# When a kernel splits its double-precision weights: ten conversions spread over the attention, and the sign joined on another engine

## The chip, the cores and the metric

The kernel runs on one core of a Trainium2 chip. Its time is the device time of one execution in microseconds (us); lower is better. The engines are named as in the profile: PE (TensorE) multiplies matrices, with its weight loads as PEld; ACT (ScalarE) evaluates functions and copies with a scale; DVE (VectorE) and POOL (GpSimd) work element by element; SP issues DMAs. Each engine works through its own list of instructions in order and waits where an operand is not ready.

## The reference, cut to what matters

```python
def _attn_ref(q, k, v, proj):                     # 2 batches x 8 heads, 768 rows of 64
    q_bucket, k_bucket = ...                      # signs of q @ proj, k @ proj, six bits each
    mask = q_bucket[:, :, :, None] == k_bucket[:, :, None, :]
    scores = np.where(mask, scale * q @ k.T, -1e9)
    attn = softmax(scores)
    return attn @ v

def _moe_ref(x, mu_k, mu_r, w_k, w_v, w_r):       # x: 2 x 768 x 512
    xk = mu_k * x + (1.0 - mu_k) * x_prev         # x_prev: x shifted by one row
    xr = mu_r * x + (1.0 - mu_r) * x_prev
    k = np.maximum(xk @ w_k, 0.0)                 # w_k: 512 x 1024
    return sigmoid(xr @ w_r) * (k * k @ w_v)

def _moe2_ref(x, U, V, w_ch1, w_ch2):
    u = x + (x.T @ U @ V).T                       # low rank, over the rows
    return u + np.maximum(u @ w_ch1, 0.0) @ w_ch2 # w_ch1: 512 x 2048
```

The weights w_k, w_v, w_r, U, V, w_ch1 and w_ch2 come in as double precision. No engine works in it, so the kernel makes single-precision numbers of them from their two 32-bit words.

## The kernel before, in words

**Attention.** Sixteen heads of six row tiles each make 96 tiles. For a tile PE makes the scores (`scores`), DVE takes the row maximum (`row_max`), ACT the exponential (`exps`, L386, tile p), ACT or DVE the upper half of the result in 16 bits (`part1`, L393 or L391) and POOL the rest (`part2`). SP then issues a transposing DMA of both halves (`transp`, pT<-p), and PE multiplies with v (`weighted`, L416). A loop over steps n goes through a table of these operations, each with an offset, and so writes every engine's list; the first exponential comes some twelve steps in. Per head, further operations prepare q and k for the head after next: loads, transposes on PE, ACT copies (L312), DVE remainders (L317), a mask of sign bits (zt), and DMAs that put the parts together (xq, xk).

**Conversions.** A list `jobs` holds 55 blocks of weights, mostly 128 x 512. One `tick()` advances a pipeline of five stages by one block each: `conv_load` (an SP DMA of 512 KB into a buffer raw, of which there are three), `conv_scale` on ACT, `conv_bits` on DVE, `conv_sum` on POOL, and `conv_split`, which gives the upper part on ACT (L206) and the remainder on DVE (L125). A block loaded in one tick is scaled in the next and split three ticks after that. Stage `conv_scale` makes three ACT passes over the pairs of words: L168 gives a scaled copy of the high word (cx); L169 puts the low word's top three bits, as a 16-bit integer, into the low half of the low word; L170 writes the high word into the other half as a 16-bit float, scaled so far down that of it only the sign bit is left. `conv_bits` shifts cx left by three, and `conv_sum` adds the word so made.

**When the ticks run.** Ten ticks run in the attention, after the steps whose number, counted from the first step, is in `TICKS`. The others run in the layers behind it: one in each block u of 384 rows (`k_half`), of which the first layer (class Mix, once per batch) has sixteen and the second (class Channel) thirty-two per batch. In such a block PE multiplies (`k`, twelve matmuls of 384 columns), ACT and POOL square the result (L586, L587, tile sq), DVE makes its remainder (`k_low`, L592, tile hl), and PE multiplies the block before it (`v`, nine matmuls of 512 columns). The tick's first half (split and sum) stands ahead of the squares, its second half (bits, scale and load) behind them and ahead of `k_low`.

Of the kernel before, what the change touches and what calls it, by code (L numbers as in the profile page):

```python
# [11 lines left out]
F16 = mybir.dt.float16  # L12
BF16 = mybir.dt.bfloat16
AF = mybir.ActivationFunctionType
ALU = mybir.AluOpType
# [7 lines left out]
P2_DVE = ()  # L23
P1_DVE = ((0, 2), (0, 5), (1, 2), (1, 5))

TICKS = (2, 5, 7, 9, 11, 12, 13, 14, 15, 17)


DRAIN = {-4: "A", -3: "pA", -2: "A", -1: "vA", 0: "pRvR", 2: "AAvpRaR", 3: "apva", 4: "aRpa", 5: "vRa", 6: "Rvpap", 8: "Ra", 9: "va", 10: "p"}
# [39 lines left out]
]  # L69
U32 = mybir.dt.uint32  # L70
I32 = mybir.dt.int32
U16 = mybir.dt.uint16
HI_SCALE = 2.0 ** -112


# [1 line left out]
def lsh_attention_moe_kernel(  # L77
# [19 lines left out]
    nc = tc.nc  # L97
# [11 lines left out]
    scale = 1.0 / float(D) ** 0.5  # L109
# [11 lines left out]
    def f(t):  # L121
        return t.bitcast(F32)
# [26 lines left out]
    live = {}  # L149
# [13 lines left out]
    def conv_scale(j):  # L163
        d = live[j]
        r, n = d["rows"], d["n"]
        d["x"] = conv_p.tile([128, 512], F32, tag="cx", name="cx", bufs=4)[0:r, 0:n]
        half = d["raw"].bitcast(U16)
        nc.scalar.activation(d["x"], f(d["raw"])[:, :, 1], AF.Copy, scale=HI_SCALE)  # L168
        nc.scalar.activation(half[:, :, 0], d["raw"][:, :, 0], AF.Copy, scale=2.0 ** -29)  # L169
        nc.scalar.activation(half[:, :, 1].bitcast(F16), f(d["raw"])[:, :, 1], AF.Copy, scale=HI_SCALE)  # L170

    def conv_bits(j):
        x = live[j]["x"].bitcast(U32)
        nc.vector.tensor_scalar(x, x, 3, None, ALU.logical_shift_left)  # L174

    def conv_sum(j):
# [14 lines left out]
    def tick_b():  # L191
        j = tick_n[0]
        tick_n[0] += 1
        stage(j - 1, conv_bits)
        stage(j, conv_scale)
        stage(j + 1, conv_load)

    def tick():
        tick_a()
        tick_b()  # L200

    def words(w):
        return w.bitcast(U32)
# [53 lines left out]
    for s in ("q", "k"):  # L257
# [4 lines left out]
        for i, a in enumerate(sgn[s]):  # L262
# [4 lines left out]
                out=rest[r, c], in0=p_raw[r], scalar=a, in1=f(both)[r, c], op0=ALU.mult, op1=ALU.subtract  # L267
# [450 lines left out]
    for n in range(first, N + lasts + 2):  # L718
# [3 lines left out]
        for kind, off, name, *a in TABLE:  # L722
# [14 lines left out]
            else:  # L737
                j, r = divmod(n - off, 2 * NT)
                if r == 0 and 1 <= j < NH // 2:
                    fns[name](j - 1, *a)  # L740
                if n == N + END[name, a[0]]:
                    fns[name](NH // 2 - 1, *a)
        if n - first in TICKS:
            tick()
# [9 lines left out]
    low = [LowRank(0, "lr"), LowRank(1, "w_c")]  # L754
# [139 lines left out]
```

## Time and profile before

| | |
|---|---|
| median of 3 runs | 794.86 us (793.02 to 802.88) |
| the profiled execution's own time | 796.41 us |
| its span in the profile | 794.6 us |
| PE busy | 693.3 us, 87% of the span |
| ACT busy | 491.5 us, 62% |
| DVE busy | 431.8 us, 54% |
| POOL busy | 320.1 us, 40% |

The attention takes the first 310 us or so, the first layer behind it runs until 510 us, and the second until the end. An engine's share of the whole span says little here, since each stage has a limit of its own; stages are to be read one by one. All stretches are given in us from the start of the span.

### The profile page before, as it was taken

The page shows a single profiled execution, that of the slowest core. Times are in us where ns is not written, and L with a number is a line of the kernel's source. Part 1 is how long each engine was busy: PE and PEld are TensorE (multiplying, and loading weights), DVE is VectorE, ACT ScalarE, POOL GpSimd, SP SyncE. Part 2 cuts the span into 40 slices and gives each one's busy share as a digit, 9 for nine tenths or more (in the row PEclk, how much of TensorE's full clock was granted, in tenths as well). Part 3 has the DMA queues.
Part 4 walks back from the last instruction along what each step waited for, and adds up shares of the span by engine and source line. Part 5 has one row for each costly group of instructions (what it writes and reads, how often), then busy time and mean ns, then how long its engine had stood idle before and what let it go on. Part 6 is the DMA issues. An engine that isn't in the chain of part 4 may idle for free.

```text
span 794.6 us, 14578 instructions
## 1 busy us (share of the span) xinstructions
PE 693.3 (87%) x5792; PEld 604.1 (76%) x5792; DVE 431.8 (54%) x811; ACT 491.5 (62%) x685; POOL 320.1 (40%) x252
## 2 busy tenths in 40 slices
PE   4458778888788887899998899999999999999997
PEld 3347667777677776688877668788899988999996
DVE  3679868887798786555684445512433333111112
ACT  7997657766677655799947999821699521111110
POOL 1457766776777674345544544321133200000000
PEclk9559989999999999999999999999999999999999
DMA  6679999999999995033201323100234002000002
GB/s 189 176 179 219 203 187 197 204 241 196 213 201 205 199 181 81 28 116 105 65 2 53 106 85 128 54 1 26 79 112 129 27 0 80 1 1 0 1 1 79
DMA packets 180291, 86.41 MB, mean 109 GB/s; under 512 B 154432, under 2 KB 172992, under 8 KB 180224
## 3 DMA queue, kind: packets, MB, share of 16 engines
q1 hardware_dynamic: 170512, 69.36, 42.9%
q10 hardware_dynamic: 9712, 16.13, 8.5%
q8 instruction: 45, 0.74, 0.4%
q14 instruction: 22, 0.18, 0.1%
HBM read 37.10 MB, written 3.15 MB: 51 GB/s over the span
## 4 chain that ended last, share of the span: by engine, by line
PE 43%; ACT 23%; DMA 12%; DVE 10%; issue 6%; POOL 3%; ACTq 2%; SPq 0%; DVEq 0%; POOLq 0%
DMA pT<-p 9%; PE ps L603 7%; PE ps L605 7%; PE ps L604 7%; PE pt L605 6%; PE pt L603 6%; PE pt L604 6%; ACT raw L169 5%; ACT p L386 4%; ACT raw L170 3%; DVE nm L372 3%; ACT cx L168 3%; ACT w L206 2%; DVE p L391 2%; POOL p L125 2%
## 5 line engine op out<-in xcount | busy, mean ns | idle before, releaser
L125 POOL TENSOR_TENSOR p<-p,p 128x768 f16<-128x768 f32 x96 | 159.2, 1661 | 71.6 <-ACT p L393 28.6
L673 ACT ACTIVATE hl<-pt 128x384 fp32r<-128x384 f32 x64 | 31.5, 493 | 169.0 <-PE pt L605 168.9
L416 PEld LDWEIGHTS <-pT 128*128 128x128 f16 x2880 | 99.9, 99 | 37.0 <-issue 28.9
L416 PE MATMUL pt<-v,pT 128*128 128x64 bf16 (+1 forms) x2880 | 110.4, 197 | 19.2 <-DVE xn L437 14.2
L674 DVE SCALAR_TENSOR_TENSOR hl<-pt,hl 128x384 fp32r<-128x384 f32 x64 | 35.6, 557 | 160.4 <-ACT hl L673 160.4
L603 PE MATMUL ps<-w,hl 128*128 128x512 f32 x288 | 115.2, 400 | 3.9 <-ACT y L573 3.3
L125 POOL TENSOR_TENSOR cx<-cx,raw 128x512 int32<-128x512 int32 (+2 forms) x55 | 77.8, 1414 | 100.0 <-DVE cx L174 85.5
L605 PE MATMUL ps<-w,hl 128*128 128x512 f32 x288 | 114.1, 396 | 4.4 <-DVE hl L592 4.4
L386 ACT ACTIVATE p<-ps,nm 128x768 f32<-128x768 f32 x96 | 94.6, 987 | 31.0 <-DVE nm L380 14.1
L604 PE MATMUL ps<-w,hl 128*128 128x512 f32 x288 | 113.3, 393 | 0.0
L367 PE MATMUL ps<-xk,xq 76*128 76x384 f32 x192 | 76.4, 398 | 23.7 <-ACT p L386 13.3
L372 DVE TENSOR_REDUCE nm<-ps 128x1 f32<-128x768 f32 x96 | 91.5, 953 | 7.5 <-PE ps L368 6.3
L125 DVE TENSOR_TENSOR w<-cx,w 128x512 fp32r<-128x512 f32 (+2 forms) x55 | 43.5, 791 | 87.7 <-ACT w L206 87.7
L603 PE MATMUL pt<-ut,w 128*128 128x384 f32 x256 | 86.5, 338 | 0.0
L605 PE MATMUL pt<-ut,w 128*128 128x384 f32 x256 | 86.1, 336 | 0.0
L604 PE MATMUL pt<-ut,w 128*128 128x384 f32 x256 | 85.9, 336 | 0.0
L170 ACT ACTIVATE raw<-raw 128x512 f16<-128x512 f32 (+2 forms) x55 | 73.8, 1342 | 1.8
L169 ACT ACTIVATE raw<-raw 128x512 uint16<-128x512 uint32 (+2 forms) x55 | 73.3, 1333 | 0.0
L605 PEld LDWEIGHTS ps<-w,hl 128*128 128x128 f32 x288 | 54.2, 188 | 20.8 <-DVE hl L592 9.2
L393 ACT ACTIVATE p<-p 128x768 f16<-128x768 f32 x64 | 54.0, 844 | 24.7 <-DMA pT<-p 20.6
L368 PE MATMUL ps<-yk,yq 128*128 128x384 f32 x192 | 69.1, 360 | 0.0
L603 PEld LDWEIGHTS ps<-w,hl 128*128 128x128 f32 x288 | 54.2, 188 | 16.9 <-ACT y L573 4.6
(123 smaller groups left out, 1290.7 us busy)
## 6 DMA issues: line engine op xcount, KB each, us to landing
raw<-in_moe_w_ch_dram SPq DMA_DIRECT2D x32, 512.0 KB
raw<-in_moe_w_k_dram SPq DMA_DIRECT2D x8, 512.0 KB
raw<-in_moe_w_v_dram SPq DMA_DIRECT2D x8, 512.0 KB
nk<-in_k_dram ACTq DMA_DIRECT2D x16, 192.0 KB
xq<-yq ACTq DMA_DIRECT2D x16, 192.0 KB
xk<-yk ACTq DMA_DIRECT2D x16, 192.0 KB
v<-in_v_dram ACTq DMA_DIRECT2D x16, 192.0 KB
nq<-in_q_dram ACTq DMA_DIRECT2D x15, 192.0 KB
```

The source lines that it names most:

```text
L125: eng.tensor_tensor(out=out, in0=a, in1=b, op=op)
L169: nc.scalar.activation(half[:, :, 0], d["raw"][:, :, 0], AF.Copy, scale=2.0 ** -29)
L170: nc.scalar.activation(half[:, :, 1].bitcast(F16), f(d["raw"])[:, :, 1], AF.Copy, scale=HI_SCALE)
L367: nc.tensor.matmul(s_ps[:, j, 0:G], d["xq"][:, qc], d["xk"][:, c], start=True, stop=False)
L368: nc.tensor.matmul(s_ps[:, j, 0:G], d["yq"][:, qc], d["yk"][:, c], start=False, stop=True)
L372: nc.vector.tensor_reduce(out=nm[:, 0:1], in_=tl[n]["s"][:, :, 0:G], axis=AX.XY, op=ALU.max, negate=True)
L386: nc.scalar.activation(p, tl[n].pop("s")[:, :, 0:G], AF.Exp, bias=nm[:, 2:3], scale=nm[:, 1:2])
L393: nc.scalar.activation(p12[:, 0], tl[n]["p"], AF.Copy)
L416: nc.tensor.matmul(o[:, 0:d], pT[:, part, kt, :], V[a][:, kt, 0:d], start=(kt == 0 and (part, a) == (0, 1)), stop=(kt == NT - 1 and (part, ...
L603: nc.tensor.matmul(o, sh, mh, start=first, stop=False)
L604: nc.tensor.matmul(o, sh, ml, start=False, stop=False)
L605: nc.tensor.matmul(o, sl, mh, start=False, stop=last)
```

## The change

Two things change. First, the ten ticks of the attention run after steps 2, 5, 8, 22, 32, and so on to 82, so three of them run in the first steps and seven are ten steps apart. Second, `conv_scale` loses its third pass. Its second pass now writes the low word's top three bits as a 32-bit integer over the low word, and a new DVE instruction at the head of `conv_bits` masks the sign out of the high word and ORs it into the low word.

```diff
-TICKS = (2, 5, 7, 9, 11, 12, 13, 14, 15, 17)
+TICKS = (2, 5, 8, 22, 32, 42, 52, 62, 72, 82)
...
-U16 = mybir.dt.uint16
...
-        half = d["raw"].bitcast(U16)
+        low = d["raw"][:, :, 0]
         nc.scalar.activation(d["x"], f(d["raw"])[:, :, 1], AF.Copy, scale=HI_SCALE)
-        nc.scalar.activation(half[:, :, 0], d["raw"][:, :, 0], AF.Copy, scale=2.0 ** -29)
-        nc.scalar.activation(half[:, :, 1].bitcast(F16), f(d["raw"])[:, :, 1], AF.Copy, scale=HI_SCALE)
+        nc.scalar.activation(low, low, AF.Copy, scale=2.0 ** -29)
...
     def conv_bits(j):
-        x = live[j]["x"].bitcast(U32)
+        x, raw = words(live[j]["x"]), live[j]["raw"]
+        nc.vector.scalar_tensor_tensor(
+            out=raw[:, :, 0], in0=raw[:, :, 1], scalar=0x80000000, in1=raw[:, :, 0],
+            op0=ALU.bitwise_and, op1=ALU.bitwise_or,
+        )
         nc.vector.tensor_scalar(x, x, 3, None, ALU.logical_shift_left)
```

The lines of the changed kernel are numbered anew: the passes are L167 and L168, the new DVE instruction is L172 and the shift L176. Lines further on are two higher than before, those of the helper L125 one lower.

On ACT, up to the second exponential (L386), these rows stand before; the conversions are L168 to L170, and L206 is the split.

```order
L325 DMA xk<-yk 64x768
L206 ACTIVATE w<-cx 128x512
L168 ACTIVATE cx<-raw 128x512
L169 ACTIVATE raw<-raw 128x512
L170 ACTIVATE raw<-raw 128x512
L386 ACTIVATE p<-ps,nm 128x768
L237 DMA v_0_126<-in_v_dram 128x384
L393 ACTIVATE p_286<-p 128x768
L312 ACTIVATE yk<-pt 64x3x128 x2
L206 ACTIVATE w<-cx 128x512
L168 ACTIVATE cx<-raw 128x512
L169 ACTIVATE raw<-raw 128x512
```

At the same place on ACT there stands now:

```order
L327 DMA xk<-yk 64x768
L388 ACTIVATE p<-ps,nm 128x768
L239 DMA v_0_126<-in_v_dram 128x384
L395 ACTIVATE p_263<-p 128x768
L314 ACTIVATE yk<-pt 64x3x128 x2
L239 DMA nk<-in_k_dram 128x384
L388 ACTIVATE p<-ps,nm 128x768
L395 ACTIVATE p_283<-p 128x768
L347 DMA xk<-zt 12x768
L388 ACTIVATE p<-ps,nm 128x768
```

No conversion stands between the first exponentials any more; three conversions, where there were five, stand ahead of the first.

On SP's list, from the mask DMA (xq<-zt) of the second head on, loads of weights (L156) and transposing DMAs (L402) take turns before:

```order
L345 DMA xq<-zt 12x768
L402 DMA_TRANSPOSE pT<-p_286 128x12x128
L156 DMA raw<-in_moe_w_v_dram 128x1024
L402 DMA_TRANSPOSE pT<-p_317 128x12x128
L156 DMA raw<-in_moe_w_k_dram 128x4x256
L402 DMA_TRANSPOSE pT<-p_366 128x12x128
L156 DMA raw<-in_moe_w_v_dram 128x1024
L402 DMA_TRANSPOSE pT<-p_385 128x12x128
```

Now, some way further on (the first eight rows from the eighth transposing DMA on, with the first moved load among them):

```order
L404 DMA_TRANSPOSE pT<-p_482 128x12x128
L404 DMA_TRANSPOSE pT<-p_580 128x12x128
L404 DMA_TRANSPOSE pT<-p_588 128x12x128
L155 DMA raw<-in_moe_w_k_dram 128x4x256
L404 DMA_TRANSPOSE pT<-p_637 128x12x128
L404 DMA_TRANSPOSE pT<-p_748 128x12x128
L347 DMA xq<-zt 12x768
L404 DMA_TRANSPOSE pT<-p_764 128x12x128
```

The seven loads have moved from places ahead of and among the first five transposing DMAs to places some ten transposing DMAs apart.

On DVE in the first layer, two blocks of batch 0 read before as follows; w<-cx,w is the split's remainder, xs_a belongs to the other batch, cx<-cx is the shift and hl<-sq,hl is `k_low`.

```order
L125 TENSOR_TENSOR w<-cx,w 128x512
L534 MEMSET xs_a 128x1
L542 TENSOR_SCALAR xs_a<-xT,omu_r 128x127
L542 TENSOR_SCALAR xs_a<-xT,omu_r 128x256
L543 SCALAR_TENSOR_TENSOR xs_a<-xT,mu_r,xs_a 128x384
L174 TENSOR_SCALAR cx<-cx 128x192
L592 TENSOR_TENSOR hl<-sq,hl 128x384
L125 TENSOR_TENSOR w<-cx,w 128x512
L174 TENSOR_SCALAR cx<-cx 32x384
L592 TENSOR_TENSOR hl<-sq,hl 128x384
```

The same two blocks on DVE now:

```order
L124 TENSOR_TENSOR w<-cx,w 128x512
L536 MEMSET xs_a 128x1
L544 TENSOR_SCALAR xs_a<-xT,omu_r 128x127
L544 TENSOR_SCALAR xs_a<-xT,omu_r 128x256
L545 SCALAR_TENSOR_TENSOR xs_a<-xT,mu_r,xs_a 128x384
L172 SCALAR_TENSOR_TENSOR raw<-raw 128x192
L176 TENSOR_SCALAR cx<-cx 128x192
L594 TENSOR_TENSOR hl<-sq,hl 128x384
L124 TENSOR_TENSOR w<-cx,w 128x512
L172 SCALAR_TENSOR_TENSOR raw<-raw 32x384
L176 TENSOR_SCALAR cx<-cx 32x384
L594 TENSOR_TENSOR hl<-sq,hl 128x384
```

One more instruction, L172, stands in each block ahead of the shift and so ahead of `k_low`.

## Rows read from the trace of the kernel before

**Rows 1.** Page, part 2: busy tenths of ACT and DMA share in forty slices.

```profile
ACT  7997657766677655799947999821699521111110
DMA  6679999999999995033201323100234002000002
```

**Rows 2.** Stretches: length, busy us (instructions) by engine, granted clock, DMA share, GB/s.

```profile
0.00:20.00 20.00, 8.12 (x26) 6.15 (x26) 7.79 (x31) 15.01 (x19) 3.42 (x11) 0.91 0.61 188
20.00:40.00 20.00, 8.24 (x28) 6.85 (x28) 13.98 (x25) 19.38 (x23) 9.56 (x7) 0.59 0.66 177
40.00:60.00 20.00, 11.30 (x87) 9.31 (x87) 15.68 (x22) 19.30 (x24) 11.95 (x9) 0.57 0.79 181
60.00:80.00 20.00, 17.63 (x298) 15.69 (x299) 18.91 (x42) 15.63 (x20) 15.12 (x12) 1.00 1.21 215
...
240.00:260.00 20.00, 16.41 (x289) 14.57 (x288) 17.61 (x39) 13.99 (x20) 13.69 (x11) 1.00 1.20 206
...
340.00:360.00 20.00, 19.48 (x94) 16.60 (x93) 12.70 (x17) 19.71 (x27) 9.19 (x10) 0.99 0.41 129
...
560.00:600.00 40.00, 40.00 (x198) 35.24 (x198) 15.39 (x30) 37.10 (x47) 11.83 (x9) 1.00 0.36 107
```

**Rows 3.** Groups by line and form: busy us, mean ns of one; idle before.

```profile
L170 ACT ACTIVATE raw<-raw 128x512 f16<-128x512 f32 x52 | 71.0, 1366 | 1.7
L169 ACT ACTIVATE raw<-raw 128x512 uint16<-128x512 uint32 x52 | 70.5, 1356 | 0.0
...
L206 ACT ACTIVATE w<-cx 128x512 fp32r<-128x512 f32 x52 | 34.7, 668 | 0.6 <-ACT yq L312 0.6
L168 ACT ACTIVATE cx<-raw 128x512 f32<-128x512 f32 x52 | 34.3, 659 | 1.2 <-DMA raw<-in_moe_w_r_dram 0.9 <-issue 0.2
```

**Rows 4.** ACT's timeline: the first, seventh and thirteenth exponential.

```profile
27.80 0.99 ACT L386 ACTIVATE p<-ps,nm 128x768 f32<-128x768 f32 x1
...
56.92 0.93 ACT L386 ACTIVATE p<-ps,nm 128x768 f32<-128x768 f32 x1
...
70.44 0.99 ACT L386 ACTIVATE p<-ps,nm 128x768 f32<-128x768 f32 x1 [0.31 <-DVE nm L380]
```

**Rows 5.** Timeline of the start: PE's first score matmul.

```profile
17.35 0.67 PE L367 MATMUL ps<-xk,xq 76*128 76x384 f32 x1
```

**Rows 6.** Page, part 4: shares of the chain that ended last.

```profile
DMA pT<-p 9%; PE ps L603 7%; PE ps L605 7%; PE ps L604 7%; PE pt L605 6%; PE pt L603 6%; PE pt L604 6%; ACT raw L169 5%; ACT p L386 4%; ACT raw L170 3%; DVE nm L372 3%; ACT cx L168 3%; ACT w L206 2%; DVE p L391 2%; POOL p L125 2%
```

**Rows 7.** ACT's timeline: starts of two successive blocks, in three stretches.

```profile
352.29 0.47 ACT L586 ACTIVATE sq<-pt 128x384 f32<-128x384 f32 x1
...
356.86 0.47 ACT L586 ACTIVATE sq<-pt 128x384 f32<-128x384 f32 x1
...
448.24 0.47 ACT L586 ACTIVATE sq<-pt 128x384 f32<-128x384 f32 x1
...
454.31 0.46 ACT L586 ACTIVATE sq<-pt 128x384 f32<-128x384 f32 x1
...
578.80 0.49 ACT L673 ACTIVATE hl<-pt 128x384 fp32r<-128x384 f32 x1
...
582.94 0.49 ACT L673 ACTIVATE hl<-pt 128x384 fp32r<-128x384 f32 x1
```

**Rows 8.** DVE instructions by line or tile: duration in ns, min/median/max.

```profile
L174 DVE TENSOR_SCALAR cx<-cx x55: 254/420/1871, 9.7 to 625.4; 128x512 uint32<-128x512 uint32 x52, 32x384 uint32<-32x384 uint32 x2, 128x192 uint32<-128x192 uint32 x1
L125 DVE TENSOR_TENSOR w<-cx,w x55: 358/693/1796, 21.0 to 629.5; 128x512 fp32r<-128x512 f32 x52, 32x384 fp32r<-32x384 f32 x2, 128x192 fp32r<-128x192 f32 x1
...
L592 DVE TENSOR_TENSOR hl<-sq,hl x32: 544/560/1664, 332.5 to 507.9; 128x384 fp32r<-128x384 f32 x32
```

**Rows 9.** PE's waits in 335 to 400 and in 425 to 470.

```profile
PE ps L603 <- ACT y L573: 3.1, 1, 3.1
PE ps L605 <- DVE hl L592: 2.2, 7, 0.4
...
PE pt L603 <- ACT sq L586: 5.2, 6, 1.2
```

## Prediction

> **What bounds the kernel now.** I read the page first, then the time by stretches, then the groups, and last the timelines of the places that the change touches. In the page the reader is to see that ACT is full in slices 2 and 3, at seven tenths or less from the fourth on, and full again in slices 18 to 20, 23 to 25, 30 and 31 [rows 1]. Each of these places holds ticks.
>
> *The first 60 us are ACT's.* Between 20 and 60 us it is busy 19.4 and 19.3 of 20 us, while the other engines and the DMAs have room [rows 2]. The first exponential starts at 27.80 although PE began its scores at 17.35 [rows 4, 5]. The first six tiles then take 29.1 us to the seventh exponential at 56.92, the next six only 13.5 [rows 4].
>
> *From 60 to 300 us it is the DMAs.* The DMA share stands near 1.2 with some 210 GB/s [rows 2] and so in every slice of that stretch [rows 1]; it can pass 1 because packets overlap, so I take 1.2 for full. The longest item of the chain, DMA pT<-p with 9% [rows 6], belongs here. ACT has 4 to 6 of 20 us free, DVE only 1 to 2.5.
>
> *The first layer is ACT's where ticks meet other ACT work, PE's elsewhere.* At 352 a block takes 4.57 us, at 448 it takes 6.07 [rows 7]. In the second layer a block with the same number of matmuls and a tick takes 4.14 with PE busy 40 of 40 us [rows 2, 7], which is what PE itself needs.
>
> **The third pass (L170).** It is 1.37 us on ACT, 55 times, 74 us in all. It counts only where ACT is last.
>
> - At 332 to 337 PE waits 3.1 us for the sigmoids, which stand behind a conversion on ACT [rows 9]: 1.4 off.
> - Blocks of batch 0 take 4.57, as the one in rows 7, against PE's 4.14; there are nine of them (338 to 381). PE's waits there are for `k_low`, 2.2 us by its own rows [rows 9]; a later square on ACT makes it late. Up to 0.43 x 9 = 3.9, none if `k_low` stays late. I take 3.
> - In batch 1 the first block has its sigmoids behind a conversion too (1.4). Four blocks take 6.07, as the one in rows 7, and PE waits 5.2 us there for L586 [rows 9]: 6.07 less 1.37 is 4.7, still above PE's 4.14 plus two matmuls of the low-rank part, so each gives 1.4 in full. Together 1.4 + 5.5 = 6.9.
> - In the second layer PE is full and the pass is worth nothing.
>
> Sum behind the attention: 1.4 + 3 + 6.9, or 11.3 us. The ends are 5, if ACT's gain is met by another engine in half of these blocks, and 15, if the other blocks with ticks shorten too.
>
> The Trainium skill (ScalarE: Activation LUTs, section "What ACT_TABLE_LOAD costs") has an ACTIVATE with immediate scale and bias at 186 ns + 0.833 ns an element whatever the type, an estimate of 0.61 us for 512 elements. L168 with 0.66 is near it; L169 and L170 with 1.36 and 1.37 are not [rows 3]. By the page the pass would be worth under half, and the 11.3 us would be some 5 to 6.
>
> **The second pass (now L168).** No row shows ACT writing 32-bit words at a step of eight bytes. It lies between 0.66 (the first pass: same input, dense output) and 1.36 (the old second pass: same step, in place, two-byte output) [rows 3]. I take 1.36, the nearer row; at 0.66 ACT would be lighter still, but PE is then last already, so it adds under 1 us.
>
> **The new DVE instruction (L172).** The nearest rows are those of DVE with two inputs in SBUF: the split's remainder, also 512 elements, with a median of 0.69 and at most 1.80 [rows 8]. I take 0.7 to 1.8. In the second layer and in batch 1 DVE is mostly idle. In the blocks of batch 0 it stands ahead of `k_low`, for whose result PE waits now [rows 9]; but its operands are a block old, so it can run while DVE waits for the squares. I cost it at nothing there beyond the 0.9 of 3.9 already left out. If that cover is gone, it costs 0.7 in each of nine blocks, which undoes the 3 us and a little more.
>
> **The moved ticks.** Seven conversions leave the first steps. Five passes stood ahead of the first exponential, three stand there now, each without the third pass. ACT's work ahead of it falls by 5 x 3.4 + 2 x 0.67 - 3 x 2.0, about 12 us [rows 3]. It cannot start much before PE's scores allow: 17.35 [rows 5] plus maximum and bias, so about 20 instead of 27.8. Behind it no conversion stands between tiles, so the next six tiles can run at 13.5 to 16 instead of 29.1. The seventh exponential comes at 34 to 39, not at 56.9: about 20 us sooner, 18 at least.
>
> The price is paid later. Between 340 and 360 us only loads run: share 0.41 for 129 GB/s [rows 2], or 315 GB/s at a share of 1, so 512 KB (524,288 bytes) cost 1.67 us. In the full stretch each load pushes the transposing DMAs behind it on SP back by 1.4 (if it packs 1.2-fold like the rest) to 1.7 us; seven cost 10 to 12. Net 20 - 11 = 9.
>
> A second route needs no start time. In the first 60 us the DMAs use (0.61 + 0.66 + 0.79) x 20 = 41 of 72 share-us, so 31/1.2 = 26 us of DMA time are empty [rows 2]. The total to move is the same afterwards. If the DMAs fill from about 26 us on, they use by then some 16 less two unissued loads, 13 of 31: 15 us empty, and up to 4 more while PE's clock and the tiles ramp up. The gain is 7 to 11. I take 8 for both routes.
>
> The rest of a moved tick must hide: on ACT 0.66 + 1.36 + 0.67 = 2.7 us, on DVE 0.7 + 0.42 + 0.69 = 1.8 [rows 3, 8], on POOL one `conv_sum`. What hides it is the DMAs being last. SP waits in each load for `conv_sum` on POOL to free a raw buffer; behind it stands the next transposing DMA, which waits for POOL's `part2` of the next tile, and that stands behind the same `conv_sum`, so the wait is not a new one. If nothing hides a tick, it costs its largest part, 2.7, and seven cost 19: the gain of 8 would be a loss of 11. I take it as hidden, with 1 us a tick as the worse end: 2 us of gain.
>
> **Sum.** 796.4 (profiled execution) - 8 - 11.3 = 777.1. That execution was 1.5 above the median of the runs, 794.9, which makes 775.6; I predict **775 us**. Two per cent, about what a measurement of this kernel can tell from no change, is 16 us: the line is at 779.
>
> **Rivals.**
>
> *The port.* Behind the attention the gain goes to a lock between DVE and POOL. `k_low` takes 0.55 alone but up to 1.66 [rows 8], and so do the shift and the remainder (maxima 1.87 and 1.80). If these are POOL's work holding DVE up, L172 adds to the contested time in every block, batch 0 stays at 4.57 and batch 1 at 5.4 or so: 4 of the 11 us are left, 783. For it: `k_low` is already what PE waits for. Against it: DVE is busy 12.7 and POOL 9.2 of 20 us at 340 [rows 2], so about 22 of 20 with the waiting counted twice, and L172 adds 3. The Trainium skill (SBUF — State Buffer, section "Who interferes with whom") states the lock: a DVE instruction with two SBUF inputs and a GpSimd instruction that reads SBUF shut each other out, the later one fully. The maxima in rows 8 fit it. Chance 0.24, with the milder case in which the moved ticks win nothing net (784).
>
> *DVE becomes the bound in the attention, and the kernel is slower.* DVE is busy 17.6 to 18.9 of 20 us there [rows 2]. A tick puts L172, shift and remainder on it, 1.8 us at the medians and 1.8 + 1.9 + 1.8 = 5.5 at the maxima [rows 8]. From (20 + 11)/7 = 4.5 a tick on, the whole gain is gone; at 5.5 the seven cost 38, and the time is 794.9 + 38 - 31 = 802. Against it: the DMAs have tiles in hand while DVE catches up, and the maxima are rare. Chance 0.05.
>
> *The loads fit between.* If the transposing DMAs leave gaps that the share does not show, the 20 us are kept and the first layer gives its 15: 760. Against it: the share is flat while every engine has room. Chance 0.10.
>
> The forecast itself has 0.61.
>
> **How the numbers follow.** The ends of the terms, 2 and 11 for the attention and 5 and 15 behind it, together make 769 to 788. The larger gain reaches on to 760, DVE's case to 802. 764 to 788 leaves out under 0.1 below and as much above. Faster by over 2% (below 779) holds most of the forecast (0.50 of 0.61), the larger gain (0.10) and a bit of the port (0.05): 0.65. Slower by over 2% (above 811) is the far end of the DVE case: 0.02. The rest, 0.33, is within 2%.
>
> **What the changed profile would show.** No L170; ACT's L168 between 0.66 and 1.36; L172 near 0.7 with some over 1.5. The seventh exponential before 40 us, the DMA share near 1.2 already from 30 us, and ACT under 16 of 20 us from 20 to 60. The attention ends some 8 us sooner. Blocks in batch 1 under 4.8 us apart, those of batch 0 near 4.2, and the second layer unchanged. The prediction is wrong if heads that hold a tick grow by over 3 us, or if `k_low` still keeps PE waiting.

## The result, and the profile after

The changed kernel takes 774.3 us (median of 4 runs, 770.4 to 782.7) where the kernel before took 797.75 beside it: ratio 0.969, 95% interval 0.959 to 0.979. In six further runs it was 774.1 against 798.95, 0.969 (0.964 to 0.975). The prediction was 775. The execution profiled first was a disturbed one, so the rows below come from one of the further runs (775.03 us, span 773.2).

Two views by line, first of the kernel before, place the gain: all exponentials, then all blocks of the first layer. Behind the count stand minimum, median and maximum in ns, then the first and the last start.

```profile
L386 ACT ACTIVATE p<-ps,nm x96: 925/992/995, 27.8 to 302.9; 128x768 f32<-128x768 f32 x96
...
L586 ACT ACTIVATE sq<-pt x32: 462/475/495, 330.4 to 505.7; 128x384 f32<-128x384 f32 x32
```

The same of the changed kernel:

```profile
L388 ACT ACTIVATE p<-ps,nm x96: 968/991/996, 18.9 to 296.5; 128x768 f32<-128x768 f32 x96
...
L588 ACT ACTIVATE sq<-pt x32: 462/491/493, 324.0 to 484.9; 128x384 f32<-128x384 f32 x32
```

The attention's last exponential comes 6.4 us sooner. From there to the first block it is 27.5 us in both. The first layer's blocks span 160.9 us instead of 175.3, 14.4 less, and what follows 288.3 instead of 288.9. Together 21.4, the difference of the two spans. The medians lie 3.5 us further apart than these two executions. In all kernels below whose first layer is the same, the blocks' span is the same to 0.1 us; what varies between these executions is the attention, so a difference of a few us there is not settled by one profile.

The page's tenths [rows 1] and the stretches [rows 2] show that ACT has left the first 60 us:

```profile
ACT  4766777667677754776547856322454221111110
...
DMA  7899999999999995033201333000343010000002
```

```profile
0.00:20.00 20.00, 10.43 (x33) 8.37 (x34) 11.24 (x37) 10.13 (x18) 2.11 (x10) 1.00 0.70 208
20.00:40.00 20.00, 16.15 (x147) 13.46 (x147) 17.66 (x35) 14.78 (x19) 13.19 (x10) 0.83 0.88 155
40.00:60.00 20.00, 15.32 (x212) 13.70 (x211) 15.39 (x31) 12.91 (x17) 13.92 (x11) 0.83 1.22 222
...
340.00:360.00 20.00, 19.60 (x100) 17.37 (x99) 19.93 (x27) 13.10 (x26) 13.29 (x10) 1.00 0.38 123
560.00:600.00 40.00, 40.00 (x204) 36.39 (x204) 32.14 (x40) 20.94 (x40) 12.11 (x10) 1.00 0.35 119
```

ACT is at 14.8 and 12.9 of 20 us where it had 19.4 and 19.3. From 340 to 360 us it falls from 19.7 to 13.1, and DVE takes its place with 19.9. At 560 PE stays full, so nothing is won there. The DMA share is near 1.2 from 40 us on, not from 30. ACT's timeline has the exponentials of [rows 4] at 18.95, 33.16 and 52.55 instead of 27.80, 56.92 and 70.44:

```profile
18.95 0.99 ACT L388 ACTIVATE p<-ps,nm 128x768 f32<-128x768 f32 x1 [1.44 <-DVE nm L382]
...
33.16 0.99 ACT L388 ACTIVATE p<-ps,nm 128x768 f32<-128x768 f32 x1 [0.32 <-DVE nm L382]
...
52.55 0.99 ACT L388 ACTIVATE p<-ps,nm 128x768 f32<-128x768 f32 x1 [2.24 <-DVE nm L382]
```

The seventh is 23.8 us sooner and the last 6.4, so 17.3 us are given back in between. The passes by group [rows 3], and DVE's instructions by line [rows 8]:

```profile
L168 ACT ACTIVATE raw<-raw 128x512 uint32<-128x512 uint32 x52 | 34.8, 669 | 0.0
L167 ACT ACTIVATE cx<-raw 128x512 f32<-128x512 f32 x52 | 34.4, 662 | 1.6 <-DMA raw<-in_moe_w_r_dram 1.3 <-DMA raw<-in_moe_w_v_dram 0.2
L208 ACT ACTIVATE w<-cx 128x512 fp32r<-128x512 f32 x52 | 32.4, 624 | 0.7 <-DMA pT<-p 0.7
```

```profile
L172 DVE SCALAR_TENSOR_TENSOR raw<-raw x55: 354/685/2137, 9.1 to 603.5; 128x512 uint32<-128x512 uint32 x52, 32x384 uint32<-32x384 uint32 x2, 128x192 uint32<-128x192 uint32 x1
...
L124 DVE TENSOR_TENSOR w<-cx,w x55: 341/1796/1865, 48.3 to 607.7; 128x512 fp32r<-128x512 f32 x52, 32x384 fp32r<-32x384 f32 x2, 128x192 fp32r<-128x192 f32 x1
```

The second pass takes 0.67 us instead of 1.36, which the prediction had only as its lower end. L172 has a median of 0.69 and reaches 2.14. The remainder's median has gone from 0.69 to 1.80. The chain that ended last [rows 6] now has DVE's share at 18% and ACT's at 4%, where it had 10% and 23%; its rows L124 and L172 are new among the larger ones. Its shares by engine before, then those by engine and by line now:

```profile
PE 43%; ACT 23%; DMA 12%; DVE 10%; issue 6%; POOL 3%; ACTq 2%; SPq 0%; DVEq 0%; POOLq 0%
...
PE 57%; DVE 18%; DMA 10%; issue 5%; ACT 4%; POOL 3%; ACTq 0%; SPq 0%; DVEq 0%; POOLq 0%
DMA pT<-p 9%; PE ps L605 9%; PE ps L607 8%; PE ps L606 8%; PE pt L607 7%; PE pt L605 7%; PE pt L606 7%; PE pt L418 4%; DVE w L124 3%; DVE nm L374 3%; POOL p L124 2%; DVE raw L172 2%; ACT p L388 2%; DVE cx L176 1%; PE ps L369 1%
```

### The profile page after: what moved, and what is told of

Its sections match the earlier page's. It is cut to its first block, busy times and chain, and to the rows that moved or that the text cites. A ratio compares the mean times of both kernels' runs of the same rounds, so it can differ in the third digit from the quotient of the medians.

```text
span 780.9 us, 14599 instructions
## 1 busy us (share of the span) xinstructions
PE 700.5 (90%) x5792; PEld 614.3 (79%) x5792; DVE 500.2 (64%) x866; ACT 390.1 (50%) x630; POOL 331.4 (42%) x252
## 4 chain that ended last, share of the span: by engine, by line
PE 57%; DVE 21%; DMA 11%; issue 5%; ACT 3%; POOL 2%; SPq 1%; ACTq 1%; DVEq 0%; POOLq 0%
PE ps L605 9%; PE ps L607 8%; PE ps L606 8%; PE pt L607 7%; PE pt L605 7%; PE pt L606 7%; DMA pT<-p 7%; DVE nm L374 4%; PE pt L418 3%; DVE w L124 3%; DVE raw L172 2%; DMA xq<-zt 2%; PE ps L334 2%; ACT p L388 2%; DVE p L393 1%
## 5 line engine op out<-in xcount | busy, mean ns | idle before, releaser
L124 POOL TENSOR_TENSOR p<-p,p 128x768 f16<-128x768 f32 x96 | 159.5, 1667 | 75.3 <-ACT p L395 24.4
L418 PEld LDWEIGHTS <-pT 128*128 128x128 f16 x2880 | 104.4, 102 | 39.1 <-issue 31.9
L418 PE MATMUL pt<-v,pT 128*128 128x64 bf16 (+1 forms) x2880 | 115.3, 200 | 21.0 <-DVE xn L439 16.3
L124 POOL TENSOR_TENSOR cx<-cx,raw 128x512 int32<-128x512 int32 (+2 forms) x55 | 79.7, 1450 | 99.5 <-DVE cx L176 62.7
L374 DVE TENSOR_REDUCE nm<-ps 128x1 f32<-128x768 f32 x96 | 91.5, 953 | 16.3 <-PE ps L370 14.8
L369 PE MATMUL ps<-xk,xq 76*128 76x384 f32 x192 | 78.8, 411 | 14.9 <-ACT p L388 7.1
L124 DVE TENSOR_TENSOR w<-cx,w 128x512 fp32r<-128x512 f32 (+2 forms) x55 | 77.8, 1415 | 13.0 <-ACT w L208 13.0
L607 PEld LDWEIGHTS ps<-w,hl 128*128 128x128 f32 x288 | 54.0, 188 | 19.3 <-DVE hl L594 7.9
L605 PEld LDWEIGHTS ps<-w,hl 128*128 128x128 f32 x288 | 54.1, 188 | 14.6 <-ACT y L575 2.2
L606 PEld LDWEIGHTS ps<-w,hl 128*128 128x128 f32 x288 | 54.1, 188 | 8.5
L369 PEld LDWEIGHTS ps<-xk,xq 76*128 76x128 f32 x192 | 40.6, 211 | 18.8 <-ACT p L388 9.9
```

What stands on the lines that cost most here:

```text
L124: eng.tensor_tensor(out=out, in0=a, in1=b, op=op)
L369: nc.tensor.matmul(s_ps[:, j, 0:G], d["xq"][:, qc], d["xk"][:, c], start=True, stop=False)
L374: nc.vector.tensor_reduce(out=nm[:, 0:1], in_=tl[n]["s"][:, :, 0:G], axis=AX.XY, op=ALU.max, negate=True)
L418: nc.tensor.matmul(o[:, 0:d], pT[:, part, kt, :], V[a][:, kt, 0:d], start=(kt == 0 and (part, a) == (0, 1)), stop=(kt == NT - 1 and (part, ...
L605: nc.tensor.matmul(o, sh, mh, start=first, stop=False)
L606: nc.tensor.matmul(o, sh, ml, start=False, stop=False)
```

## The experiments

My theory was the prediction's: the start of the attention and the first layer, each by its own part of the change, less the price of seven loads. Against it stood the lock of DVE and POOL, DVE as the bound in the attention, and that the parts share one gain. "Last" is the start of the last exponential, "blocks" the span from the first to the last square as above; each ratio is against the kernel before on the same chip. That kernel took 798.95 us beside e0, e1, e2 and e4, 797.15 beside e3, e5, e6 and e9, 798.21 beside e7, e8 and e10, and 795.32 beside e11, so medians from different chips differ by a few us without any edit. "Last" and "blocks" come from one execution each. In e3 that execution took 793.2 us, in e5 774.6, in e7 769.6 and in e10 781.3, each 3 to 4 us off its median; the others are within 2 us, and the kernel before's, from an earlier run, took 796.4. The runs of one kernel spread over 5 to 14 us, so I take a median as good to about 2 us, an estimate.

| kernel | median us | ratio (95%) | last | blocks |
|---|---|---|---|---|
| before (profile) | 798.95 | 1 | 302.9 | 175.3 |
| e0_changed_again | 774.1 | 0.969 (0.964 to 0.975) | 296.5 | 160.9 |
| e1_ticks_alone | 792.8 | 0.992 (0.988 to 0.996) | 300.8 | 175.2 |
| e2_sign_alone | 776.1 | 0.974 (0.968 to 0.979) | 298.9 | 160.9 |
| e4_loads_first | 771.0 | 0.965 (0.961 to 0.970) | 292.3 | 160.9 |
| e3_extra_loads | 789.1 | 0.990 (0.984 to 0.996) | 315.6 | 160.9 |
| e9_tick_twice | 787.2 | 0.990 (0.986 to 0.993) | 309.6 | 161.0 |
| e10_dve_twice | 785.5 | 0.984 (0.978 to 0.990) | 304.1 | 160.9 |
| e5_low_two_bytes | 777.8 | 0.975 (0.969 to 0.981) | 296.4 | 162.0 |
| e6_no_sign | 767.5 | 0.963 (0.959 to 0.968) | 292.4 | 158.7 |
| e7_low_ahead | 773.6 | 0.968 (0.964 to 0.973) | 288.6 | 164.3 |
| e8_square_ahead | 785.0 | 0.983 (0.978 to 0.988) | 295.2 | 172.7 |
| e11_or_on_dve | 766.3 | 0.966 (0.961 to 0.970) | 289.7 | 158.8 |

**The changed kernel again** (e0).

> The changed kernel once more, nothing left out, for a profile of an undisturbed execution. Prediction's sum: attention 8 us shorter (last exponential near 295 instead of 302.9), the first layer 11 to 15 us shorter (first square to the second layer's start 165 to 169 us instead of 180.6), 772 to 777 us in all. Rival (the first layer alone pays): last exponential at 301 to 304 and a first layer 20 us shorter, the same total.

As expected, with 1.5 us less in the attention than the sum had it. The rival, that the first layer alone pays, is out.

**Each part alone.** e1 is the kernel before with the new `TICKS`, e2 the changed kernel with the old:

```diff
-TICKS = (2, 5, 8, 22, 32, 42, 52, 62, 72, 82)
+TICKS = (2, 5, 7, 9, 11, 12, 13, 14, 15, 17)
```

> The kernel before with the new places of the ten ticks alone; each conversion keeps its three ACT passes. My theory (the ticks are worth 8 us in the attention, and each later tick, hidden under the DMAs, costs nothing more by its third pass): 785 to 790 us, the seventh exponential near 38, the first layer as before (180 us). Rival A (a tick in the full stretch costs its load and its passes on ACT, 1.7 + 3.4 us, seven times 36 us against 20 won): 800 to 812. Rival B (loads fit between, the 20 us are kept): 775 to 778.

> The changed kernel with the ten ticks at their old places: the sign on DVE and the 32-bit second pass alone. In the first layer 15 us less (165.6 us instead of 180.6), as far as the changed kernel showed it. In the first 60 us, where ACT was full, each conversion is 3.40 - 1.33 = 2.06 us lighter on ACT; eight or nine of them lie ahead of the seventh exponential, so that comes 16 to 18 us sooner, near 40, with no load moved into the full stretch. If the parts don't add up in this way because both serve the same 20 us: 763 to 770, at or below the whole change (then the moved ticks are worth nothing beside the sign, or cost a little). If the moved ticks' 8 us are a gain of their own: 780 to 784.

The ticks alone win 6.1 us of the medians, the sign alone 22.9, both 24.9. The first layer's gain is wholly the sign's: 160.9 and 175.2. e1 was a miss: 792.8 lies between my 785 to 790 and the 800 of rival A, though its seventh exponential came even sooner than I had said, so what is given back behind it is larger:

```profile
35.36 0.99 ACT L386 ACTIVATE p<-ps,nm 128x768 f32<-128x768 f32 x1 [0.31 <-DVE nm L380]
```

At the start of the attention the two share one gain: the seventh exponential is 21.6 us sooner in e1, 8.4 in e2, and 23.8 with both. For the attention as a whole it is not settled. Beside the sign the moved ticks are worth 2.0 us by the medians, where they are worth 6.1 alone, but the intervals of e0 and e2 overlap, and the last exponentials (2.1 and 4.0 us sooner alone, 6.4 together) show no sharing. e2 fell between my two cases, for its seventh exponential came at 48.5, not near 40. Its stretches suggest why: DVE, which now has three instructions of each early conversion, takes ACT's place as the fullest engine.

```profile
20.00:40.00 20.00, 10.86 (x36) 8.85 (x36) 17.97 (x32) 15.24 (x23) 12.34 (x9) 0.76 0.78 210
40.00:60.00 20.00, 14.65 (x188) 12.87 (x188) 19.28 (x34) 14.26 (x20) 14.68 (x11) 0.73 1.10 193
```

**The price of a load** (e4, e3). e4 sends four of the seven loads early, into buffers where the first layer's inputs lie later; e3 sends each of the seven twice. Their diffs, in this order:

```diff
+        p, b = (early_p, 4) if 4 <= j < 8 else (conv_p, 3)
...
+        if n - first in range(9, 13):
+            conv_load(n - first - 5)
```

```diff
         if n - first in TICKS:
             tick()
+            if n - first > 8:
+                extra_load()
```

> The changed kernel with four of the moved ticks' loads (the fifth to the eighth of all) sent right behind the fourth load, ahead of the first transposing DMA, into four buffers of their own; passes and ticks stay where they are. If a load in the full stretch costs what the prediction took (1.4 to 1.7 us each), the last exponential comes 5 to 7 us sooner: 766 to 769. If loads fit between the transposing DMAs, or the attention is not the DMAs' any more: no change, 773 to 776. If the four loads delay the first tiles: up to 7 us of start lost, 774 to 781.

> The changed kernel with the load of each of the seven moved ticks sent twice, the second time into a buffer that nobody reads; passes once. Priced by the four loads that were sent early (3.1 us of the medians, 4.2 of the last exponentials, so 0.8 to 1.05 each), seven more cost 5.5 to 7.5: 779.5 to 781.5, the last exponential at 302 to 304. By the prediction's 1.4 to 1.7 each: 784 to 786. If loads fit between the transposing DMAs: 774 as the changed kernel.

e4's last exponential is 4.2 us sooner than e0's, 1.05 a load, less than expected. Only 1.5 of it is there at the 49th exponential (155.1 and 156.6), behind all four loads; the rest comes where both kernels send the same loads, so a price from this one pair of executions is loose. e3's last is 19.1 later, 2.7 a load, but that is e3's slowest execution; its median is 15.0 above e0's, 2.1 a load. Either is more than the 1.4 to 1.7 of the prediction, though e3's four runs (782.6 to 793.2) are too spread out to exclude the upper end of that.

The low price in e4 and the high one in e3 would agree if what counts is how long the DMAs are empty, by the prediction's second route: with 1.2 for full, the first 60 us leave (3.6 - 2.80) x 20 / 1.2 = 13 us empty in e0 and, with shares of 0.72, 1.12 and 1.14, 10 us in e4. A load that moves into them wins only what it fills, here 3 us. This is argued and not shown: the same sum gives 26 - 13 = 13 us for the whole change, and the attention gained 6.4 us by the profiles and 9.9 by the medians (24.9 less the 15.0 behind the attention).

A load more costs about its bytes at the full stretch's own rate. From 60 to 280 us e3 moves 206 GB/s, beside the 207 of the row of e0 below, so the rate did not rise when loads were added:

```profile
60.00:280.00 220.00, 169.70 (x2530) 150.63 (x2530) 173.42 (x340) 142.31 (x190) 144.10 (x100) 0.88 1.19 206
```

Seven loads are 3.67 MB and take 17.8 us at that rate, between the 15.0 and the 19.1; at the 315 GB/s that the prediction took from a stretch of loads alone they would take 11.7.

e4's stretches, for the shares:

```profile
0.00:20.00 20.00, 9.82 (x34) 8.00 (x35) 11.24 (x37) 9.88 (x17) 2.11 (x10) 0.91 0.72 222
20.00:40.00 20.00, 15.61 (x130) 13.54 (x129) 17.39 (x33) 14.51 (x20) 13.90 (x10) 0.74 1.12 234
40.00:60.00 20.00, 13.94 (x200) 12.28 (x197) 15.83 (x30) 12.71 (x18) 13.42 (x10) 0.83 1.14 210
```

**The rest of a late tick** (e9, e10). e9 does the seven ticks' work on ACT, DVE and POOL twice, e10 DVE's three instructions alone. Of the stage on bits, the others likewise:

```diff
+        for i in again():
             nc.vector.scalar_tensor_tensor(
...
-        nc.vector.tensor_scalar(x, x, 3, None, ALU.logical_shift_left)
+            nc.vector.tensor_scalar(x, x, 0 if i else 3, None, ALU.logical_shift_left)
```

> The changed kernel in which the engines' work of the seven moved ticks is done twice (three ACT passes, three DVE instructions, the POOL sum, each repeated so that the result stays the same), with one load each. If the work of a tick is hidden under the DMAs, as the prediction took it: 774 to 776. At the 1 us a tick that it named as the worse end: 781. If nothing hides it, the largest part, 2.0 us on ACT or 1.8 and more on DVE, counts: 787 to 790, and DVE's case by its maxima would be 800 or more.

> The changed kernel in which DVE's three instructions of each of the seven moved ticks alone are done twice. Everything of a tick twice had cost 13 us. If that is DVE's part (1.8 us at the medians and up to 5.5 held up by POOL, ahead of the maximum and the conversion of the next tiles): 784 to 788. If it was ACT's three passes or POOL's second sum: 774 to 777. In between, both share it.

A second dose is not hidden: it costs 13.1 us, and 11.4 of it by the medians (7.6 against 13.1 by the last exponentials, in e10's fastest execution) come with DVE's part alone. From 60 to 280 us the rows of e0 and then of e9 fit this: the DMAs' share and rate fall as DVE's 182 of 220 us become 194, so in e9 the DMAs are no longer kept as full.

```profile
60.00:280.00 220.00, 174.65 (x2783) 154.73 (x2780) 182.15 (x372) 154.44 (x204) 155.54 (x109) 0.95 1.19 207
```

```profile
60.00:280.00 220.00, 172.43 (x2667) 155.28 (x2666) 194.39 (x372) 158.12 (x215) 157.76 (x108) 0.88 1.12 197
```

One such tick in e0, on DVE and then on POOL:

```profile
136.70 1.30 DVE L124 TENSOR_TENSOR w<-cx,w 128x512 fp32r<-128x512 f32 x1 [0.64 <-ACT w L208]
137.92 2.12 DVE L172 SCALAR_TENSOR_TENSOR raw<-raw 128x512 uint32<-128x512 uint32 x1
...
140.30 0.94 DVE L374 TENSOR_REDUCE nm<-ps 128x1 f32<-128x768 f32 x1
...
141.60 0.55 DVE L393 CAST p<-p 128x768 f16<-128x768 f32 x1
```

```profile
137.39 2.10 POOL L124 TENSOR_TENSOR p<-p,p 128x768 f16<-128x768 f32 x1
142.23 1.64 POOL L124 TENSOR_TENSOR p<-p,p 128x768 f16<-128x768 f32 x1 [2.73 <-DVE rl L426]
```

L172 takes 2.12 us while POOL's `part2` runs beside it. Behind it wait the next row maximum and the conversion at 141.60, and behind them POOL, which is idle for 2.73 us until the DVE instruction that follows the conversion (tile rl).

**The second pass** (e5).

```diff
+        half = d["raw"].bitcast(mybir.dt.uint16)[:, :, 0]
-        nc.scalar.activation(low, low, AF.Copy, scale=2.0 ** -29)
+        nc.scalar.activation(half, low, AF.Copy, scale=2.0 ** -29)
```

> The changed kernel with the second pass writing two bytes at a step of eight again, as before the change (1.36 us a pass instead of 0.67); DVE's new instruction stays in number and size but with a mask of the low word in place of the sign (the sign is left out, so the weights come out without it). By the prediction a faster second pass was worth under 1 us, so this would be 774 to 775. By what the changed trace shows (the first two blocks of each batch, 3.7 and 4.0 us shorter, have two conversions ahead of the sigmoids, each 1.37 + 0.69 lighter): 1.4 us come back in each batch, and up to 2 more at the start of the attention: 777 to 779, the first layer 168.5 instead of 165.7.

The edit shown is the ACT pass; DVE's new instruction masks the low word instead, so e5 leaves the sign out. The pass is back at two bytes and double the time:

```profile
L169 ACT ACTIVATE raw<-raw 128x512 uint16<-128x512 uint32 x52 | 71.1, 1368 | 0.0
```

The blocks span 1.1 us more, less than the 2.8 expected: the first two blocks of the batches are 1.0 and 1.3 longer, and part of that is made up in the blocks behind, where DVE's remainder is held up less (median 1.33 us, in e0 1.80). The medians give 3.7, or 0.5 without e5's longest run, the intervals overlap, and the last exponential is where it was. The faster second pass is worth 1.1 us net in the first layer; whether it is worth more elsewhere stays open.

**The new DVE instruction** (e6 leaves L172 out and with it the sign; e7 and e8, on top of e4, move `k_low`; e11, on top of e4, drops POOL's sum). The edit of e6, then those of e7 and e8 in `k_half`:

```diff
-        nc.vector.scalar_tensor_tensor(
-            out=raw[:, :, 0], in0=raw[:, :, 1], scalar=0x80000000, in1=raw[:, :, 0],
-            op0=ALU.bitwise_and, op1=ALU.bitwise_or,
-        )
```

```diff
-        if tick:
-            tick_b()
         mix.k_low(u)
+        if tick:
+            tick_b()
```

```diff
-        if tick:
-            tick_a()
         mix.k_act(u)
+        if tick:
+            tick_a()
...
-        if tick:
-            tick_b()
         mix.k_low(u)
+        if tick:
+            tick_b()
```

> The changed kernel without the new DVE instruction (the sign is left out, so the weights come out without it). In the changed trace batch 0's blocks from 358 to 381 are 4.83, 4.58, 4.81, 4.59 and 4.31 us apart against 4.13 ahead of them, with DVE full; L172 takes 0.69 to 1.31 there. If it is the cause (the port rival, in the place where it is left): these blocks come to 4.14 to 4.3, the first layer to 163.5, the time to 771 to 772.5. If the remainder held up by POOL (1.8 us) and the shifts fill the blocks without it: 773 to 775, blocks above 4.5. In the attention I expect nothing of it, since the DMAs are last; if DVE were last there, seven to ten times 0.7 or more would go: 766 to 769.

Batch 0's blocks from 358 to 377 start 4.58 to 4.83 us apart in e0, and 4.13 in e6; three starts of the one and two of the other, from ACT's timelines:

```profile
362.94 0.49 ACT L588 ACTIVATE sq<-pt 128x384 f32<-128x384 f32 x1 [1.73 <-PE pt L607]
367.52 0.49 ACT L588 ACTIVATE sq<-pt 128x384 f32<-128x384 f32 x1 [1.90 <-PE pt L607]
372.34 0.49 ACT L588 ACTIVATE sq<-pt 128x384 f32<-128x384 f32 x1 [2.23 <-PE pt L607]
```

```profile
357.43 0.49 ACT L584 ACTIVATE sq<-pt 128x384 f32<-128x384 f32 x1 [1.04 <-PE pt L603]
361.56 0.49 ACT L584 ACTIVATE sq<-pt 128x384 f32<-128x384 f32 x1 [1.45 <-PE pt L603]
```

So L172 makes these blocks late and costs 2.2 us of the first layer, which is what the port rival said of it. The held-up remainder alone does not make them late, for in e6 it still takes 1.8 us in most of them:

```profile
360.74 1.79 DVE L124 TENSOR_TENSOR w<-cx,w 128x512 fp32r<-128x512 f32 x1
```

The last exponential was 4.1 sooner too, which I had not expected and which agrees with DVE being nearly last there, though one pair of executions does not settle it.

> The kernel with four loads sent first, and in the first layer k_low stands on DVE ahead of the tick's two instructions on bits instead of behind them (ACT's passes and the next load move behind it in the order too). If k_low's place behind L172 is what slows batch 0's blocks (4.82, 4.59, 4.81, 4.58, 4.31 us), they come to 4.13 as without L172: batch 0 takes 88 us instead of 89.8, the time is 768.5 to 769.5. Rival: the order closes a loop, bits, POOL's sum, POOL's square, k_low and the bits again, of 0.69 + 0.42 + 1.55 + 1.28 + 0.55 = 4.5 us by the undisturbed durations and up to 5.9 by the held-up ones; then every block with a tick that PE could do in 4.14 takes 4.5 to 5.9, the first layer grows by 4 to 15 us, 775 to 786.

> As the one with k_low ahead of the bits, and ACT's relu and square and POOL's square stand ahead of the tick's copy, remainder and sum too. That opens the loop: POOL's sum of a tick no longer stands ahead of the square for which k_low waits. Expected: batch 0's blocks at 4.13 to 4.3, batch 0 at 88 us, the heads of both batches as they are or up to 0.7 us shorter, second layer unchanged, 768 to 769.5. Rival: the lock of DVE and POOL is what costs, wherever the instructions stand: blocks stay at 4.5 to 4.8, 771.

e7 went as its rival: the blocks alternate between 4.77 and 4.89, and the layer grows by 3.4 us. In the waits from 338 to 392 us the loop is to be seen, POOL's sum waiting for the bits and `k_low` for the square:

```profile
POOL cx L124 <- DVE cx L180: 15.8, 9, 2.3
DVE hl L598 <- POOL sq L124: 11.8, 7, 2.0
```

e8 was a miss: 11.8 us longer in the first layer than e4. A later sum frees the raw buffer later, so in the same stretch ACT waits for a load that neither case had:

```profile
ACT cx L171 <- DMA raw<-in_moe_w_k_dram: 8.2, 4, 3.0
```

The order as it stands is the best of the three. e11 takes the sum away from POOL instead (and rounds the second pass down, so that the OR is right):

```diff
-        nc.vector.tensor_scalar(x, x, 3, None, ALU.logical_shift_left)
-
-    def conv_sum(j):
-        x = live[j]["x"].bitcast(I32)
-        two(nc.gpsimd, x, x, live[j]["raw"].bitcast(I32)[:, :, 0], ALU.add)
+        nc.vector.scalar_tensor_tensor(
+            out=x, in0=x, scalar=3, in1=raw[:, :, 0], op0=ALU.logical_shift_left, op1=ALU.bitwise_or,
+        )
```

> The kernel with four loads sent first, in which POOL's sum of each conversion is gone: DVE's shift ORs the low word in with it (two inputs, as L172), and the second pass rounds down so that the low word stays below 8. DVE gets longer by some 0.27 us a tick (0.69 for 0.42), POOL loses 1.3 to 1.6. If it is POOL's work that holds DVE's two-input instructions up (the lock) and the chain of bits, sum and square that makes k_low late: batch 0's blocks at 4.13, batch 0 at 88.0 and the first layer at 163.4 us as without L172, L172 and the remainder nearly all near 0.69, the attention 2 to 5 us shorter, 764 to 767. If DVE's own total is what counts, 17 ticks in a row with 0.27 more make 0 to 3 us: 771 to 774, blocks as before at 4.6 to 4.8.

The blocks span 158.8 us, as without L172, though DVE does more. Remainder and L172 (here L125 and L177) are back at 0.69:

```profile
L125 DVE TENSOR_TENSOR w<-cx,w x55: 347/685/1744, 49.1 to 597.6; 128x512 fp32r<-128x512 f32 x52, 32x384 fp32r<-32x384 f32 x2, 128x192 fp32r<-128x192 f32 x1
...
L177 DVE SCALAR_TENSOR_TENSOR raw<-raw x55: 353/683/1317, 9.0 to 593.3; 128x512 uint32<-128x512 uint32 x52, 32x384 uint32<-32x384 uint32 x2, 128x192 uint32<-128x192 uint32 x1
```

So it was POOL's sum that held the remainder up. The Trainium skill (SBUF — State Buffer, section "Who interferes with whom") has such a lock between a DVE instruction with two SBUF inputs and a GpSimd instruction that reads SBUF; the fall of the remainder's median from 1.80 to 0.69 agrees with it. Without the sum POOL also comes to the square sooner, for which `k_low` waits, so e11 does not say whether that or the shorter remainder brought the blocks back. e4 and e11 are the fastest kernels here with nothing left out, by 0.4% against the changed one; that difference is within the intervals, and the ratios do not tell e11 from e4. What rows show is 2.1 us in the blocks for e11 and 4.2 of one pair of profiles for e4.

## Why the prediction was right

The time was right, and the gain came from the two places named, but the agreement to 1 us is luck in part. The prediction subtracted 8 + 11.3 = 19.3 us from a first median of 794.9; the kernel before then had medians of 797.75 and 798.95, and the change won 23.5 and 24.9 from them. Inside the attention a larger start met a larger price, and the step that hid the late ticks' work failed.

- *The first layer*, 11.3 predicted, 14.4 measured. ACT's timeline before gives the first three blocks of batch 0:

```profile
330.42 0.49 ACT L586 ACTIVATE sq<-pt 128x384 f32<-128x384 f32 x1 [0.99 <-PE pt L605]
...
338.53 0.49 ACT L586 ACTIVATE sq<-pt 128x384 f32<-128x384 f32 x1
...
343.13 0.49 ACT L586 ACTIVATE sq<-pt 128x384 f32<-128x384 f32 x1
```

And in e0:

```profile
324.01 0.49 ACT L588 ACTIVATE sq<-pt 128x384 f32<-128x384 f32 x1 [0.99 <-PE pt L607]
...
330.40 0.49 ACT L588 ACTIVATE sq<-pt 128x384 f32<-128x384 f32 x1
333.01 0.46 ACT L588 ACTIVATE sq<-pt 128x384 f32<-128x384 f32 x1
```

12.7 us have become 9.0, so 3.7, and in batch 1, read likewise, 4.0. The prediction counted one third pass at each head, 1.4, and had the second block of batch 0 among its nine. PE's wait for the first sigmoids has fallen from 3.1 us [rows 9] to 1.1, by more than the 1.37 of a third pass. There are two conversions, ACT is last through both, and each is 1.37 + 0.69 lighter. PE's timeline has the wait:

```profile
327.13 0.50 PE L605 MATMUL ps<-w,hl 128*128 128x512 f32 x1 [1.13 <-ACT y L575]
```

The four blocks of 6.07 gave what they should, 1.3 to 1.5 each and 5.65 together, 5.5 predicted; with the other blocks the rest of batch 1 is 5.4 shorter. The rest of batch 0 gave 1.3, since L172 keeps `k_low` late in five blocks; the prediction had named this as the cover that may be gone. 7.7 + 5.4 + 1.3 = 14.4. By whole batches it is 5.0 against 4.4 predicted and 9.4 against 6.9, so most of what was missed is the second block of batch 1, 2.0 us, which the prediction had at nothing.
- *The second pass* was taken at 1.36 and took 0.67. "Under 1 us" for it was a little low: 1.1 in the first layer by e5. The rule of the Trainium skill (ScalarE: Activation LUTs, section "What ACT_TABLE_LOAD costs") gives an estimate of 0.61 us for 512 elements, and the section says it for fp32 and bf16 alike, which is less than the prediction's "whatever the type". The 0.67 now is near it, e5's 1.37 for 16-bit integers is not. That the third pass would be worth under half by it did not come true: each block of 6.07 lost about the 1.37 of a pass.
- *The attention*, 8 predicted, 6.4 by the profiles and 9.9 by the medians. The start was 23.8 sooner at the seventh exponential, not 20. It was credited to the moved ticks, and e1 has 21.6 with them alone; but e2 shows that the sign without them gains as much by the end, 7.9 of the 9.9, by giving back less. The price was 17.3 by the profiles and near 14 by the medians, instead of 10 to 12: 2.0 to 2.5 a tick instead of 1.6.
- *The price's two steps failed.* A load costs 2.1 to 2.7 us when it comes on top (e3), not 1.4 to 1.7, and a second dose of the engines' work of a late tick, which was taken as hidden, costs 1.9 (e9), most of it DVE's (e10). The two prices together would be 28 to 32 us, more than was given back, so a first dose is partly covered; how the price divides stays open. The heads with a tick did grow by over 3 us, as the prediction named for its failure: worked out from the starts of every sixth exponential from the seventh on, a head takes 20.0 us with a late tick and 14.8 without, 16.1 before. Seven heads with 3.9 more and seven with 1.3 less make about the 17.3 given back; what outweighs them is the start.
- *The rivals.* The port's lock shows in the durations (e11), but L172 cost 2.2 us of the first layer (e6), not 7. DVE's case had the right engine at a price of 1.1 to 1.6 a tick instead of 4.5. Its 17.6 to 18.9 of 20 us, and the "1 to 2.5" free, were read from two stretches; from 60 to 280 us DVE had 182 of 220 before the change as well. Loads that fit between are excluded by e3.
- *The marks.* The second layer is unchanged, as said. Batch 1's blocks are 4.60 to 4.87 us apart, but most later ones 5.03 to 5.36, above the 4.8 named; four of these had been 4.57 to 4.60, and without L172 (e6) they are the same, so what lengthened them stays open. The other mark of failure came too: `k_low` still keeps PE waiting, from 328 to 395 us no less than the 2.2 before [rows 9]:

```profile
PE ps L607 <- DVE hl L594: 2.7, 6, 0.9
```

## What to carry to other kernels

Two edits that relieve the same full engine in the same stretch need not add up: here their gains at the start of the attention overlapped (21.6 and 8.4 us alone, 23.8 together), while the whole times left it open. So price the second one in the profile that the first would leave. In a stretch where the DMAs are full, price a transfer that comes in by its bytes at that stretch's own rate. When an engine with few idle microseconds takes work over, count what it is held up by beside its own durations, and who is queued behind it.

## What the runs showed of the hardware

ACT takes 1.37 us for 512 two-byte results at a step of eight bytes and 0.67 for four-byte results at the same step, in place and from the same input (e5 and e0). One POOL instruction of 1.3 to 1.6 us per conversion raised the median of DVE's remainder from 0.69 to 1.80 us (e11 and e4, which has e0's 1.80). The instruction alone does not do it: with it in place the kernel before had 0.69 too, and so has e7, which has the instructions of e4 in another order. One remainder of e7 and one of e0, both among the blocks of batch 0:

```profile
362.86 0.69 DVE L124 TENSOR_TENSOR w<-cx,w 128x512 fp32r<-128x512 f32 x1
```

```profile
363.39 1.79 DVE L124 TENSOR_TENSOR w<-cx,w 128x512 fp32r<-128x512 f32 x1
```

So the order of the lists can decide whether DVE is held up. That it does so by the moment at which the two meet is argued, not shown, since that moment was not varied by itself.
